# Two-block attention: the parts of the first block's row maxima made by three sums over one tile

## The chip, the cores and the metric

The kernel runs on one core of one Trainium2 chip. The core has a matrix engine (TensorE; PE in the profile, PEld for its weight loads), a vector engine (VectorE, DVE), a scalar engine (ScalarE, ACT), a general engine (GpSimd, POOL), and a queue engine (SyncE, SP) that here issues all transfers. The metric is the device time of one execution in microseconds; the median of the runs is compared.

## What is computed

Two independent attention layers, A and B, each on x of 2048 x 512 float32 with 32 heads of 16. A attends causally within a window of 256 tokens, B to all tokens. Cut to what matters:

```
scores = q @ k^T / sqrt(16)                    # per head, 2048 x 2048
A only: scores = where(0 <= i - j < 256, scores, -1e9)
p = softmax(scores);  o = p @ v;  result = o @ wo
out = concat(A's result, B's result) along the last axis
```

## The kernel before

Block 0 (A) and block 1 (B) are each cut into units (b, g, c): 8 groups g of 4 heads by 4 chunks c of 512 query tokens, 32 units a block. For each unit there are four kinds of work.

First the row maxima. `max_item` multiplies queries and keys for two heads into two PSUM banks and DVE reduces them. In block 0 that is, for a tile of 128 queries, a masked copy inside PSUM (L509) and a reduction over 256 keys (L510), or for the first two query tiles a fused operation for each head (L505). In block 1 it is a reduction over 512 keys (L457). The maxima go to a tile `mt`, allocated by `maxima` from a pool of three.

Second, `max_finish` turns the 16 maxima of a row of partitions (4 heads by 4 query tiles) into three bf16 parts whose sum is the negative maximum to float32 accuracy: part 0 is -m rounded, part 1 is what is left, rounded, part 2 is what is left after that. In block 0, and for the first unit of block 1, DVE does this with four operations (L562 to L565) through a float32 tile `nr`; the later 31 units of block 1 do it on POOL (L559, L560, L564, L565). The parts stand in one of two tiles `nmt` of 128 x 2 x 32 bf16, of which 24 columns of each half are used.

Third, `max_rows`: TensorE transposes the parts into PSUM (L579), ACT copies them to SBUF (`ntr`, L581), and two transfers (L586) write them as three extra rows under the queries in `oq`. The keys carry three rows of ones there, so the next product subtracts the maximum by itself.

Fourth, `scores` (L612) multiplies keys and queries with these rows, ACT takes the exponential (L619), POOL zeroes masked corners in block 0 (L629), and `weigh` or `weigh2` (L658, L643) multiplies with the values.

Block 0 also holds the projections of both layers (L212, L340): their results go through ACT (L295), through POOL (L305, L306) and out to DRAM; key and query loads (L370, L386) bring them back by head. POOL also splits weights and inputs (L162).

The order of PE's work in block 0 is a string written out by hand, `ORDER_A`, one letter for each piece: "m" a `max_item`, "t" a `max_rows`, "s" scores, "w" weighing, "g" and "p" projections, "e" maxima of block 1 made ahead. Around it runs a planner, `Model`: it keeps a time for each engine, for each PSUM bank and for the transfers, adds a planned duration for each piece (`M.run("DVE", 1360)` in `max_finish`), chooses PSUM banks by when they are planned to be free, and slots loads and the follow-up work of DVE and POOL into the program where the planned PE time reaches their due time. A unit's last "m" must come after the "t" of the unit before. Block 1 runs on a repeated pattern of the same letters with a fixed step.

Of the kernel before, what the change touches and what calls it, by code (L numbers as in the profile page):

```python
# [11 lines left out]
F32 = mybir.dt.float32  # L12
F32R = mybir.dt.float32r
BF16 = mybir.dt.bfloat16
AF = mybir.ActivationFunctionType
ALU = mybir.AluOpType
AX = mybir.AxisListType
# [3 lines left out]
HG = 4  # L21
# [121 lines left out]
def attention_kernel(ctx: ExitStack, tc: tile.TileContext, xT, wqk, wv, wo, out):  # L143

    nc = tc.nc
    ctx.enter_context(tc.manual_schedule())

    cst = ctx.enter_context(tc.tile_pool(name="cst", bufs=1))
    sb = ctx.enter_context(tc.tile_pool(name="sb", bufs=2))
# [3 lines left out]
    M = Model()  # L153
    ready = {}
    obank = [None]
    ns = 0
    xs, ws, parts, vd, opq, mt, pts, pvt, od, rl, osp = {}, {}, {}, {}, {}, {}, {}, {}, {}, {}, {}
# [84 lines left out]
    mone = cst.tile([128, 2, 128], BF16, name="mone")  # L242
    later = mone.bitcast(mybir.dt.uint16)
    junk = cst.tile([128, 256], BF16, name="junk")
    nmt = [cst.tile([128, 2, 32], BF16, name=f"nm{i}") for i in range(2)]
    opk = [cst.tile([128, HG // 2, S], F32R, name=f"opk{i}") for i in range(2)]
    vt = [cst.tile([128, NT, VP + 16 * i], F32, name=f"vt{i}") for i in range(2)]
    vst = [cst.tile([128, H, VW], F32, name=f"vst{i}") for i in range(2)]
# [4 lines left out]
    def constants():  # L253
        make_identity(nc, ident)
        nc.gpsimd.memset(minus, -1.0)
        nc.gpsimd.memset(wmask, 0.0)
        nc.gpsimd.affine_select(out=wmask[:, 128:], in_=wmask[:, 128:], pattern=[[-1, 128]],
                                compare_op=ALU.is_ge, fill=NEG, base=0, channel_multiplier=1)
        nc.gpsimd.memset(mone, 1.0)
        nc.gpsimd.affine_select(out=mone, in_=mone, pattern=[[0, 2], [1, 128]], compare_op=ALU.is_ge,  # L260
                                fill=zero_fill, base=-1, channel_multiplier=-1)
        nc.vector.memset(ps_all[:, 0], 0.0)
        for v in vst:
            nc.gpsimd.memset(v, 1.0)
        for v in nmt:
            nc.gpsimd.memset(v, 0.0)
        nc.gpsimd.memset(vt[1][:, :, VP:], 1.0)

# [164 lines left out]

    def maxima(b, g, c):

        if (b, g, c) not in mt:
            m = sb.tile([128, NQC, HG, 4], F32, name=f"mt_{b}_{g}_{c}",
                        **(dict(tag="mte", bufs=1) if (b, g, c) == (1, 0, 0) else dict(tag="mt", bufs=3)))
            mt[b, g, c] = m.rearrange("p k h q -> p h q k")
        return mt[b, g, c]  # L440
# [41 lines left out]
    def max_item(b, g, c, qt, j, kc):  # L482
        n = f"{b}_{g}_{c}_{qt}_{j}_{kc}"
        if b:
            banks, two = take2()
            release2(banks, max2(g, c, qt, kc, (j, j + 1), two))
            return
        m = maxima(b, g, c).rearrange("p (a r) q k -> p a r q k", a=2)
        r = j // 2
        i = 4 * c + qt  # L490
        follow(("k", b, g))
        follow(("q", b, g, c))


        t0, t1 = 128 * max(i - 2, 0), 128 * (i + 1)
        w = t1 - t0
        banks, two = take2()
        for a in range(2):
            rows = slice(ROW[a], ROW[a] + KS)
            nc.tensor.matmul(two[:, a, 0:w], opq[b, g, c][rows, r, 128 * qt:128 * qt + 128], opk2(g)[rows, r, t0:t1],  # L500
                             start=True, stop=True)
        t = M.pe("h", 20 + w / 2.4, loaded(b, g, c))
        if i < 2:
            for a in range(2):
                op = nc.vector.tensor_tensor_reduce(junk[:, :w], two[:, a, 0:w], wmask[:, 256 - w:], 1.0, -3.0e38,  # L505
                                               ALU.add, ALU.max, accum_out=m[:, a, r, qt, 0:1])
                t = M.run("DVE", w / 0.96 + 310, t)
        else:
            nc.vector.copy_predicated(two[:, :, 256:384], later, two[:, :, 0:128])  # L509
            op = nc.vector.tensor_reduce(out=m[:, :, r, qt, 0], in_=two[:, :, 128:384], axis=AX.X, op=ALU.max)  # L510
            M.run("DVE", 455, t)
            t = M.run("DVE", 610)
        release2(banks, mark(op, t))

    def max_chunk(b, g, c, kc):

        n = f"{b}_{g}_{c}"
        m = mt[b, g, c]
        if kc == 1:
            parts["mm"] = sb.tile([128, HG, 4], F32, name=f"mm_{n}", tag="mm")  # L520
        mm = parts["mm"]
        x = m[:, :, :, kc]
        up = sb.tile([128, HG, 4], F32, name=f"mu_{n}_{kc}", tag="mu", bufs=1)
        gt = sb.tile([128, HG, 4], F32, name=f"mg_{n}_{kc}", tag="mg", bufs=1)

        if kc == 1:
            nc.gpsimd.tensor_sub(up, x, m[:, :, :, 0])  # L527
        else:
            nc.gpsimd.tensor_add(up, x, mm)
        nc.gpsimd.tensor_scalar(gt, up, 0.0, None, op0=ALU.is_gt)  # L530
        nc.gpsimd.tensor_mul(up, up, gt)
        if kc == 1:
            nc.gpsimd.tensor_add(up, up, m[:, :, :, 0])
            nc.gpsimd.tensor_scalar(mm, up, -1.0, None, op0=ALU.mult)
        else:
            nc.gpsimd.tensor_sub(mm, mm, up)
        return mm

    def max_finish(b, g, c):

        n = f"{b}_{g}_{c}"
        eng = nc.gpsimd if slot[0] else nc.vector
        m = mt[b, g, c]
        if b == 0:
            mr = m[:, :, :, 0]
        else:
            if slot[0]:
                mr = max_chunk(b, g, c, 3)
            else:
                mr = sb.tile([128, HG, 4], F32, name=f"mm_{n}", tag="mm")  # L550
                nc.vector.tensor_reduce(out=mr, in_=m, axis=AX.X, op=ALU.max)

        nmt.reverse()
        parts["nm"] = nmt[0]
        nm = [nmt[0][:, :, 8 * i:8 * i + 8] for i in range(3)]
        r1 = sb.tile([128, HG, 4], F32, name=f"nr_{n}", tag="nr")
        mr, r1 = (x.rearrange("p (a r) q -> p a (r q)", a=2) for x in (mr, r1))
        if slot[0]:
            eng.tensor_copy(nm[0], mr)  # L559
            eng.tensor_sub(r1, mr, nm[0])  # L560
        else:
            nc.vector.tensor_scalar(nm[0], mr, -1.0, None, op0=ALU.mult)  # L562
            nc.vector.scalar_tensor_tensor(r1, mr, -1.0, nm[0], op0=ALU.mult, op1=ALU.subtract)
        eng.tensor_copy(nm[1], r1)  # L564
        eng.tensor_sub(nm[2], r1, nm[1])  # L565
        ready["nm", b, g, c] = M.run("DVE", 1360)

    def max_rows(b, g, c):
        n = f"{b}_{g}_{c}"
        nm = parts["nm"]  # L570
        if slot[0]:

            bank = M.take("e")
            ps = view(bank)
        else:
            bank, ps = room()
        ps = ps.bitcast(BF16)
        for a in range(2):
            nc.tensor.transpose(ps[32 * a:32 * a + 32, :128], nm[:, a], ident)  # L579
        nt = sb.tile([64, 128], F32, name=f"ntr_{n}", tag="ntr")  # L580
        op = nc.scalar.activation(nt, ps[:64, :128], AF.Copy)  # L581
        t = mark(op, M.run("ACT", 200, M.pe("c", 80)))
        release(bank, t)
        for a in range(2):
            ready["q", b, g, c] = M.dma(12, t)
            nc.sync.dma_start(opq[b, g, c][ROW[a] + KS:ROW[a] + KM].bitcast(F32).rearrange(  # L586
                "s r (q t) -> s (r q) t", t=128), nt[32 * a:32 * a + 24])


    def steps_of(c):  # L590
# [223 lines left out]
    slot = [False, 0]  # L814
# [166 lines left out]
    nm = k = nb = ne = 0  # L981
# [20 lines left out]
    while todo_a or gen[0]:  # L1002
        settle()
        pe = M.t["PE"]
        tl, name = loads()
# [4 lines left out]
        x = "p" if gen[0] else todo_a[0]  # L1010
# [4 lines left out]
        i, j = divmod(ns, HG)  # L1015
        t = NEVER
        if gen[0]:
            t = pe
        elif x == "p":
            t = max(bank(), operands(its_a[nb]))  # L1020
        elif x == "g" and stage == 0:
            t = max(bank(1), operands(its_a[nb]), operands(its_a[nb + 1], int(its_a[nb][0] == its_a[nb + 1][0])))
        elif x == "g":
            t = min(since)[0] if CHUNK * stage == 12 else pe
        elif x == "t" and nts:
            t = max(ready["nm", *nts[0]] + LOAD, bank())
        elif x == "w" and k < i:
            un, (m, pieces), a, z = flat[k]
            t = max(*(ready.get(("v", 0, un[1] // 2, y[0]), NEVER) for y in pieces), ready["p", *un, m] + 100,
                    M.bank("o") if a else 0)  # L1030
        elif x == "s" and i < k + AHEAD and (max_rows, *flat[i][0]) in made:
            t = max(bank(1), ready["q", *flat[i][0]] + LAND)
        elif x == "e":
            t = max(ready.get(("qe",), NEVER), ready.get(("ke", early[ne][2]), NEVER)) + LAND + 1500
            t = max(t, M.pair(), M.t["DVE"] - 300)
        elif x == "m" and not (mxs[nm][2] and (nts or mxs[nm][0][0] and ne < len(early))):
            un, it, z = mxs[nm]
            t = max(*(ready.get(("k", *un[:2], c), NEVER) for c in (range(NQC) if un[0] else range(un[2] + 1))),
                    ready.get(("qd", *un), NEVER)) + LAND
            t = max(t, M.pair())  # L1040
# [25 lines left out]
        elif x == "w":  # L1066
            un, st, a, z = flat[k]
# [74 lines left out]
    ns, nq, nm, half, got = 0, -8, AHEADM, 0, 0  # L1142
# [3 lines left out]
    while nq < 4 * len(steps):  # L1146
# [3 lines left out]
        for x in ORDER if nm < len(mx) else LAST:  # L1150
            k = ns // HG
            if x == "s" and k < len(steps):
                if ns % HG == 0:
                    t = k * STEP
# [88 lines left out]
```

## Time and profile before

| | us |
|---|---|
| median of 3 runs | 1824.5 (1822.27 to 1826.25) |
| the profiled execution | 1817.65 |
| its span, first to last instruction | 1815.8 |
| busy: PE | 1797.3 |
| busy: DVE | 1532.4 |
| busy: ACT | 1398.6 |
| busy: POOL | 648.4 |

The profile is of one execution, with a granted TensorE clock of 0.997 of full speed. A row "PEld x <- DVE y" in a list of waits means that a weight load for x waited for the DVE operation y. In a timeline, the columns are start and duration in us, engine, line, operation, output and input, count, and in brackets the idle time before and what ended it. Matmuls are pipelined and their ends are modelled, so PE counted as busy can still be held back a little.

### The profile page before, as it was taken

To read this page: it belongs to the slowest core of one execution; us is meant where nothing else is said; L and a number is where in the kernel's file an instruction comes from. 1 tells how busy PE (TensorE), PEld (TensorE's weight loads), DVE (VectorE), ACT (ScalarE), POOL (GpSimd) and SP (SyncE) were. 2 spreads that over 40 slices of the span, in tenths; PEclk is the share of its full clock that TensorE was granted. 3 is DMA by queue.
4 is the path that set the end of the run, shared out by engine and by line. 5 is a ranking of instruction groups with operands and counts; after the bars stand their busy time and mean duration, and the time that the engine had idled before them with its cause. 6 is when DMAs were issued, how large, how long until landed. Compare 5 with 4: busy or idle time off the path is not lost.

```text
span 1815.8 us, 39073 instructions
## 1 busy us (share of the span) xinstructions
PE 1797.3 (99%) x14982; PEld 913.6 (50%) x14982; DVE 1532.4 (84%) x2276; ACT 1398.6 (77%) x2750; POOL 648.4 (36%) x1334
## 2 busy tenths in 40 slices
PE   9999999999999999999999999999999999999999
PEld 6776566767764445444444444444444444444436
DVE  5667786777879777799999999999999999999901
ACT  4365666655558777799999999999989999999983
POOL 0367877764654332033310023320112422022330
PEclk9999999999999999999999999999999999999999
DMA  7765667544573221311200221130031121010012
GB/s 246 216 187 201 202 197 224 169 154 145 162 208 105 81 86 55 89 35 40 61 28 27 53 55 29 29 78 16 16 76 34 29 63 37 17 54 11 29 37 93
DMA packets 129162, 166.80 MB, mean 92 GB/s; under 512 B 23012, under 2 KB 58852, under 8 KB 128964
## 3 DMA queue, kind: packets, MB, share of 16 engines
q1 hardware_dynamic: 128976, 164.31, 30.2%
q8 instruction: 118, 1.93, 0.5%
q14 instruction: 68, 0.56, 0.1%
HBM read 94.49 MB, written 68.19 MB: 90 GB/s over the span
## 4 chain that ended last, share of the span: by engine, by line
PE 95%; DVE 2%; ACT 1%; DMA 1%; issue 0%; SPq 0%; POOL 0%; ACTq 0%; DVEq 0%
PE ps_all L643 30%; PE ps_all L453 20%; PE ps_all L612 19%; PE ps_all L212 13%; PE ps_all L340 6%; PE ps_all L658 4%; PE ps_all L500 3%; DVE mt L510 1%; ACT p L619 1%; DVE ps_all L509 0%; DVE mt L457 0%; PE ps_all L579 0%; DMA in<-xT_A 0%; DVE nm L562 0%; DMA opk<-parts 0%
## 5 line engine op out<-in xcount | busy, mean ns | idle before, releaser
L619 ACT ACTIVATE p<-ps_all 128x512 f32<-128x512 f32 x2432 | 1257.9, 597 | 188.2 <-PE ps_all L612 133.3
L457 DVE TENSOR_REDUCE mt<-ps_all 128x2 f32<-128x1024 f32 x1516 | 1195.0, 873 | 62.2 <-PE ps_all L453 55.0
L612 PE MATMUL ps_all<-oq,opk 51*128 51x512 f32 (+2 forms) x2752 | 774.0, 406 | 4.7 <-ACT p L619 2.6
L453 PE MATMUL ps_all<-opk,oq 48*128 48x512 f32 x2016 | 676.1, 439 | 0.4 <-DVE mt L457 0.3
L643 PE MATMUL ps_all<-p,vt 128*17 128x256 f32 (+1 forms) x6056 | 588.6, 461 | 0.6 <-ACT ou L669 0.5
L612 PEld LDWEIGHTS ps_all<-oq,opk 51*128 51x128 f32 x2752 | 398.7, 185 | 183.6 <-ACT p L619 156.2
L453 PEld LDWEIGHTS ps_all<-opk,oq 48*128 48x128 f32 x2016 | 309.7, 185 | 317.4 <-DVE mt L457 179.4
L629 POOL TENSOR_SCALAR_AFFINE_SELECT p<-p 128x256 f32<-128x256 f32 x480 | 178.6, 407 | 109.9 <-ACT p L619 103.7
L643 PEld LDWEIGHTS ps_all<-p,vt 128*17 128x17 f32 x6056 | 100.7, 95 | 223.7 <-issue 213.0
L527 POOL TENSOR_TENSOR mu<-mt 128x16 f32<-128x16 f32 x31 | 6.8, 220 | 508.0 <-DVE mt L457 508.0
L509 DVE COPY_PREDICATED ps_all<-mone,ps_all 128x256 f32<-128x256 uint16 x224 | 95.1, 425 | 82.8 <-PE ps_all L500 80.2
L510 DVE TENSOR_REDUCE mt<-ps_all 128x2 f32<-128x512 f32 x224 | 155.2, 693 | 7.7
L697 POOL TENSOR_TENSOR rd<-ld,minus 128x32 f32<-128x32 f32 x15 | 81.9, 5458 | 219.5 <-DMA ld<-od 219.5
L340 PE MATMUL ps_all<-x,w 64*128 64x512 f32 x672 | 119.3, 392 | 0.0
L212 PE MATMUL ps_all<-x,w 128*128 128x512 f32 x432 | 108.8, 400 | 1.3 <-ACT x L161 1.0
L500 PE MATMUL ps_all<-opk,oq 48*128 48x384 f32 (+2 forms) x512 | 95.1, 370 | 5.0 <-DVE mt L510 2.1
L658 PE MATMUL ps_all<-p,vt 128*17 128x384 f32 (+2 forms) x1408 | 96.4, 389 | 0.0
L212 PE MATMUL ps_all<-w_o,x_o 128*128 128x512 f32 x384 | 92.6, 396 | 0.0
L212 PEld LDWEIGHTS ps_all<-x,w 128*128 128x128 f32 x432 | 78.6, 188 | 24.2 <-issue 3.0
L340 PEld LDWEIGHTS ps_all<-x,w 64*128 64x128 f32 x672 | 85.8, 185 | 6.6 <-ACT raw L295 0.3
L295 ACT ACTIVATE raw<-ps_all 128x512 f32<-128x512 f32 x56 | 32.5, 597 | 72.5 <-PE ps_all L212 55.9
L212 PEld LDWEIGHTS ps_all<-w_o,x_o 128*128 128x128 f32 x384 | 70.6, 188 | 29.6 <-issue 12.8
(82 smaller groups left out, 980.1 us busy)
## 6 DMA issues: line engine op xcount, KB each, us to landing
parts<-st SPq DMA_DIRECT2D x64, 512.0 KB
oq<-parts SPq DMA_DIRECT2D x128, 128.0 KB
opk<-parts SPq DMA_DIRECT2D x128, 128.0 KB
od<-ou SPq DMA_DIRECT2D x64, 256.0 KB
vd<-vst SPq DMA_DIRECT2D x32, 272.0 KB
oq<-parts SPq DMA_DIRECT2D x128, 64.0 KB
opk<-parts SPq DMA_DIRECT2D x128, 64.0 KB
t<-od SPq DMA_DIRECT2D x32, 256.0 KB
```

What stands on the lines that cost most here:

```text
L212: nc.tensor.matmul(ps, l(u), r(v), start=start and k == 0, stop=stop and k == n - 1)
L340: op = nc.tensor.matmul(view(banks[a ^ turn]), l(u)[rows], r(v)[rows], start=turn == q == 0, stop=turn == 1 and q == 11)
L453: nc.tensor.matmul(ps[:, n], q[rows, 128 * qt:128 * qt + 128], k[rows, kc * QC:kc * QC + QC], start=True, stop=True)
L457: op = nc.vector.tensor_reduce(out=m[:, a:a + len(heads), r, qt, kc], in_=ps, axis=AX.X, op=ALU.max)
L500: nc.tensor.matmul(two[:, a, 0:w], opq[b, g, c][rows, r, 128 * qt:128 * qt + 128], opk2(g)[rows, r, t0:t1], start=True, stop=True)
L509: nc.vector.copy_predicated(two[:, :, 256:384], later, two[:, :, 0:128])
L510: op = nc.vector.tensor_reduce(out=m[:, :, r, qt, 0], in_=two[:, :, 128:384], axis=AX.X, op=ALU.max)
L612: nc.tensor.matmul(ps[x][:, col:col + n1], opk2(g)[rows, pr, 128 * k:128 * k + 128], opq[b, g, c][rows, pr, q0:q0 + n1], start=True, stop= ...
L619: op = nc.scalar.activation(p[:, a0 + x, :w], ps[x][:, :w], AF.Exp, scale=SCALE)
L629: nc.gpsimd.affine_select(out=v, in_=v, pattern=[[0, 2], [sign, 128]], compare_op=ALU.is_ge, fill=zero_fill, base=base, channel_multiplier ...
L643: nc.tensor.matmul(o[32 * j:32 * j + VW, q0:q1], vt[(g // 2) % 2][:, kt, vc:vc + VW], pts[1, g, c, kt, j // 2][:, j % 2, q0:q1], start=kt ...
L658: nc.tensor.matmul(o[32 * j:32 * j + VW, q0:q0 + w], vt[(g // 2) % 2][:, kt, vc:vc + VW], pts[b, g, c, m, j // 2][:, j % 2, col:col + w], ...
```

## The change

For block 0, `maxima` no longer allocates a tile of its own: the maxima are written into the first of four slots of a float32 tile `xt` (two of them, used in turn, of 128 x 2 halves x 4 slots x 8). The three parts are bf16 and are written into the upper half-words of the other three slots, whose lower half-words were zeroed once, so that each slot, read as float32, is exactly its part. On DVE part i is then one reduction: the negated sum over slots 0 to i, rounded to bf16. The 31 units of block 1 that finish on POOL keep their four operations and only write into the slots. The transposes read the upper half-words of all four slots (32 columns, every second half-word), and the two transfers take rows 8 to 31 of each half in place of 0 to 23. The planned duration of a finish goes from 1360 to 620 ns.

```diff
-    nmt = [cst.tile([128, 2, 32], BF16, name=f"nm{i}") for i in range(2)]
+    xt = [cst.tile([128, 2, 4, 2 * HG], F32, name=f"nm{i}") for i in range(2)]
...
     def maxima(b, g, c):
 
+        if not b:
+            if (b, g, c) not in mt:
+                xt.reverse()
+                mt[b, g, c] = xt[0]
+            return mt[b, g, c].rearrange("p a s (r q) -> p a r q s", q=4)
...
-        m = maxima(b, g, c).rearrange("p (a r) q k -> p a r q k", a=2)
+        m = maxima(b, g, c)
...
     def max_finish(b, g, c):
 
         n = f"{b}_{g}_{c}"
-        eng = nc.gpsimd if slot[0] else nc.vector
-        m = mt[b, g, c]
-        if b == 0:
-            mr = m[:, :, :, 0]
+        if b:
+            xt.reverse()
+        x = xt[0] if b else mt[b, g, c]
+        parts["nm"] = x
+        nm = x.bitcast(BF16).rearrange("p a s (n u) -> p a n s u", u=2)[:, :, :, :, 1]
+        if slot[0]:
+            mr = max_chunk(b, g, c, 3)
+            r1 = sb.tile([128, HG, 4], F32, name=f"nr_{n}", tag="nr")
+            mr, r1 = (y.rearrange("p (a r) q -> p a (r q)", a=2) for y in (mr, r1))
+            nc.gpsimd.tensor_copy(nm[:, :, :, 1], mr)
+            nc.gpsimd.tensor_sub(r1, mr, nm[:, :, :, 1])
+            nc.gpsimd.tensor_copy(nm[:, :, :, 2], r1)
+            nc.gpsimd.tensor_sub(nm[:, :, :, 3], r1, nm[:, :, :, 2])
         else:
-            if slot[0]:
-                mr = max_chunk(b, g, c, 3)
-            else:
-                mr = sb.tile([128, HG, 4], F32, name=f"mm_{n}", tag="mm")
-                nc.vector.tensor_reduce(out=mr, in_=m, axis=AX.X, op=ALU.max)
-
-        nmt.reverse()
-        parts["nm"] = nmt[0]
-        nm = [nmt[0][:, :, 8 * i:8 * i + 8] for i in range(3)]
-        r1 = sb.tile([128, HG, 4], F32, name=f"nr_{n}", tag="nr")
-        mr, r1 = (x.rearrange("p (a r) q -> p a (r q)", a=2) for x in (mr, r1))
-        if slot[0]:
-            eng.tensor_copy(nm[0], mr)
-            eng.tensor_sub(r1, mr, nm[0])
-        else:
-            nc.vector.tensor_scalar(nm[0], mr, -1.0, None, op0=ALU.mult)
-            nc.vector.scalar_tensor_tensor(r1, mr, -1.0, nm[0], op0=ALU.mult, op1=ALU.subtract)
-        eng.tensor_copy(nm[1], r1)
-        eng.tensor_sub(nm[2], r1, nm[1])
-        ready["nm", b, g, c] = M.run("DVE", 1360)
+            if b:
+                nc.vector.tensor_reduce(out=x[:, :, 0], in_=mt[b, g, c].rearrange("p (a r) q k -> p a (r q) k", a=2),
+                                        axis=AX.X, op=ALU.max)
+            x = x.rearrange("p a s n -> p a n s")
+            with nc.allow_low_precision(reason="a part is what is left, rounded; the sum is float32"):
+                for i in range(3):
+                    nc.vector.tensor_reduce(out=nm[:, :, :, i + 1], in_=x[:, :, :, 0:i + 1], axis=AX.X, op=ALU.add,
+                                            negate=True)
+        ready["nm", b, g, c] = M.run("DVE", 620)
 
     def max_rows(b, g, c):
         n = f"{b}_{g}_{c}"
-        nm = parts["nm"]
+        nm = parts["nm"].bitcast(BF16).rearrange("p a s (n u) -> p a (s n) u", u=2)[:, :, :, 1]
...
-                "s r (q t) -> s (r q) t", t=128), nt[32 * a:32 * a + 24])
+                "s r (q t) -> s (r q) t", t=128), nt[32 * a + 8:32 * a + 32])
```

More of the change, by code (lines that the diff above doesn't have):

```diff
@@ L264, in constants @@
             nc.gpsimd.memset(v, 1.0)
-        for v in nmt:
+        for v in xt:
             nc.gpsimd.memset(v, 0.0)
```

## The prediction

> **What bounds the kernel now.** I read the page first: the span, then the chain that ended last.
>
> ```profile
> span 1815.8 us, 39073 instructions
> ...
> PE 95%; DVE 2%; ACT 1%; DMA 1%; issue 0%; SPq 0%; POOL 0%; ACTq 0%; DVEq 0%
> ```
>
> TensorE (PE) sets the end, so DVE time is worth something only where PE stands waiting for it. The changed lines run on DVE 33 times, from 46.7 to 521.6 us. I therefore read the windows by stretch next: the first block, and the later half of the second.
>
> ```profile
> 45.00:525.00 480.00, 470.73 (x4193) 329.73 (x4193) 350.17 (x740) 278.66 (x566) 321.22 (x621) 1.00 0.60 188
> 1130.00:1735.00 605.00, 604.66 (x5207) 245.56 (x5203) 597.98 (x771) 547.05 (x1071) 148.89 (x351) 1.00 0.14 37
> ```
>
> Columns: stretch, length, busy PE, PEld, DVE, ACT, POOL, then the granted clock. In the first block PE is idle 480.00 - 470.73 = 9.27 us and DVE has 130 us free. In the second PE is idle 0.34 us in 605 although DVE is full (597.98); there the parts are made on POOL. So only the first block can gain, and not much. The waits say for whom: the PEld rows are those of 45 to 525 us, the PE rows those of 45 to 530:
>
> ```profile
> PEld ps_all L612 <- ACT p L619: 13.1, 27, 1.1
> PEld ps_all L500 <- ACT p L619: 9.4, 27, 1.0
> PEld ps_all L500 <- DVE mt L510: 7.6, 19, 0.9
> PE ps_all L500 <- DVE mt L510: 2.1, 5, 0.6
> PE ps_all L612 <- DVE mt L510: 0.7, 2, 0.5
> PE ps_all L612 <- DVE mt L457: 0.6, 1, 0.6
> PEld ps_all L500 <- DVE nm L565: 1.1, 3, 0.4
> PEld ps_all L612 <- DVE nm L565: 0.7, 2, 0.4
> ```
>
> The numbers are the total, the count and the longest in us. A weight load waits (PEld) until a PSUM bank is free; PE itself goes idle only once the earlier matmuls have drained. Idle PE is therefore the low reading of a stall and waiting PEld the high one. DVE is one of two suppliers of banks; ACT is the other.
>
> **The four operations removed.** Their rows, grouped by line and shape:
>
> ```profile
> L562 DVE TENSOR_SCALAR nm<-mt 128x16 bf16<-128x16 f32 x32 | 13.1, 409 | 1.2
> L565 DVE TENSOR_TENSOR nm<-nr,nm 128x16 bf16<-128x16 f32 x33 | 11.1, 336 | 1.1
> L563 DVE SCALAR_TENSOR_TENSOR nr<-mt,nm 128x16 f32<-128x16 f32 x32 | 9.8, 306 | 1.1
> L564 DVE CAST nm<-nr 128x16 bf16<-128x16 f32 x33 | 8.9, 271 | 1.1
> ...
> L551 DVE TENSOR_REDUCE mm<-mt 128x16 f32<-128x64 f32 x1 | 0.3, 269 | 0.0
> ```
>
> 409 + 306 + 271 + 336 = 1322 ns for a unit. The view by tile gives the spread of one of them (shortest, median, longest in ns):
>
> ```profile
> L564 DVE CAST nm<-nr x33: 174/176/1137, 47.2 to 520.2; 128x16 bf16<-128x16 f32 x33
> ```
>
> An operation of 174 ns that can take 1137 waits for something, and the surplus is a wait that shows in no wait row. The timeline of the last of the 33 shows it:
>
> ```profile
> 518.29 1.29 POOL L306 TENSOR_TENSOR st<-raw,st 128x512 fp32r<-128x512 f32 x1
> 518.73 0.27 DVE L551 TENSOR_REDUCE mm<-mt 128x16 f32<-128x64 f32 x1
> 519.04 0.57 DVE L562 TENSOR_SCALAR nm<-mm 128x16 bf16<-128x16 f32 x1
> ...
> 520.21 1.30 POOL L306 TENSOR_TENSOR st<-raw,st 128x512 fp32r<-128x512 f32 x1
> 520.40 1.15 DVE L565 TENSOR_TENSOR nm<-nr,nm 128x16 bf16<-128x16 f32 x1
> ```
>
> Both removed operations shown end 0.03 to 0.04 us after the POOL instruction that was running when they began: L562 at 519.61 behind one ending at 519.58, L565 at 521.55 behind 521.51. The one reduction from SBUF, L551, began and ended inside a POOL instruction and took 0.27: it was not held.
>
> **The three sums added.** No row shows a sum over SBUF. They read 16, 32 and 48 elements a partition and write 16. From below each costs the 174 ns of the smallest operation; from above the 269 ns of L551, which reads 64 with a stride. Near that row, I take 200, 220 and 240 ns: 660 for a unit, with ends 522 and 807. Starts stand about 0.04 us after ends in these rows, so the chain is 4 x 0.04 + 1.32 = 1.48 us before and 3 x 0.04 + 0.66 = 0.78 after. That is 0.70 us a unit, 23 us of DVE time over 33 units, most of it lying in DVE's free 130 us.
>
> The Trainium skill bears on the row L551: the page SBUF — State Buffer, section "Who interferes with whom", says that on trn2 a tensor_reduce never contends with GpSimd for the port the two share, while scalar operations and casts can, and an operation with two SBUF inputs does against a GpSimd instruction that reads SBUF. By that rule the sum is as it stands; by its opposite it is that of the third rival. This case's trace agrees with the rule at its one reduction (0.27 us under a POOL instruction).
>
> **What of it lies on the path.** I looked along the chain of waits for the removed lines. They are on it as a run four times, the last being the one shown (519.04 to 521.55 us). For the other three, the chain's first row and its first after the run, or its last:
>
> ```profile
> 168.29 1.07 DVE nm L562
> ...
> 170.35 0.43 DVE ps_all L509
> ...
> 241.67 0.19 DVE nm L562
> ...
> 243.81 0.35 DVE ps_all L509
> ...
> 338.50 1.08 DVE nm L562
> ...
> 340.37 0.27 DVE nm L565
> ```
>
> The weight loads that came late behind them:
>
> ```profile
> 171.55 0.19 PEld L500 LDWEIGHTS ps_all<-opk,oq 48*128 48x128 f32 x2 [0.60 <-DVE mt L510]
> ...
> 172.61 0.19 PEld L500 LDWEIGHTS ps_all<-opk,oq 48*128 48x128 f32 x2 [0.87 <-DVE mt L510]
> ...
> 243.96 0.19 PEld L612 LDWEIGHTS ps_all<-oq,opk 51*128 51x128 f32 x2 [0.35 <-DVE nm L565]
> ...
> 244.93 0.19 PEld L500 LDWEIGHTS ps_all<-opk,oq 48*128 48x128 f32 x2 [0.79 <-DVE mt L510]
> ...
> 342.64 0.30 PEld L612 LDWEIGHTS ps_all<-oq,opk 51*128 51x128 f32 x4 [0.85 <-DVE mt L510]
> ```
>
> For the fourth, the waits of 515 to 530 us:
>
> ```profile
> PEld ps_all L612 <- DVE mt L457: 0.9, 1, 0.9
> PEld ps_all L453 <- DVE nm L562: 0.4, 1, 0.4
> ```
>
> By waiting PEld the four stalls are 1.47, 1.14, 0.85 and 1.3 us. The runs of removed operations are 2.06, 2.14, 2.14 and 2.51 us; less 0.78 each, the change takes away 1.28, 1.36, 1.36 and 1.73. The smaller of each pair adds to 1.28 + 1.14 + 0.85 + 1.3 = 4.6 us. By PE's own idle time all stalls on DVE in the block are 2.1 + 0.7 + 0.6 = 3.4 us; I put four fifths of it, 2.7, behind these runs as the low end. Elsewhere L565 holds weight loads for 1.1 + 0.7 - 0.35 = 1.45 us; I count a quarter, 0.4. Sum: 5.0 us, with 2.7 and 6.1 as ends if nothing else moves.
>
> **The rest, at nothing.** The maxima of a unit now land in one of two tiles that the parts share; a unit's first maximum must not overwrite parts that TensorE still has to transpose. The source keeps the transposes of a unit ahead of the last maximum of the next in PE's order, so that wait is over before it is asked. The transposes read every second half-word in place of a dense row:
>
> ```profile
> L579 PEld LDWEIGHTS <-nm 128*32 128x32 bf16 x128 | 6.5, 94 | 18.0 <-POOL nm L565 12.0 <-issue 4.4
> ...
> L559 POOL CAST nm<-mm 128x16 bf16<-128x16 f32 x31 | 6.1, 197 | 2.1
> L534 POOL TENSOR_SCALAR mm<-mu 128x16 f32<-128x16 f32 x31 | 8.0, 258 | 2.7
> ```
>
> Element counts stay. In the second block POOL makes the same four operations with a strided output: if each rose from the 197 ns of the cheapest row to the 258 of the dearest POOL row of that shape, that is 4 x 61 = 244 ns in 31 units, 7.6 us, and the transposes do wait there for POOL (12.0 us). I take 0, as these rows look like a fixed cost per instruction; nothing suggests a gain. For the transposes of both blocks I take 0 by their own row: the same 128x32 a load. Doubled, 94 ns on 128 loads are 12 us of weight loading, but PEld is busy only 329.73 of 480 us and loads ahead of PE, so a tenth of it, 1 us, is the upper end. The two transfers of the rows start at partition 8 in place of 0, at equal size: 0. The planner now counts 620 ns in place of 1360 for a finish. PE's list in the first block is written out, but loads, subtractions and stores are slotted in, and PSUM banks chosen, by the planner's clock. They will move a little in either direction; I take 0 and keep the bounds in the rivals.
>
> The profiled execution took 1817.65 us (span 1815.8, 1.85 around it), so by its own time the sum is 1812.65. It lies 6.9 below the median 1824.5 of the runs shown; off that median: 1819.5.
>
> **Rivals.** *More comes free, 1813.* Each finish ends 0.7 us earlier also where DVE's delay reaches PE only after several maxima. All weight-load waits on mt in L500 are 7.6 us, of which 1.47 + 0.79 = 2.3 are in the sum; freeing the other 5.3 and the rest of L565's gives 5.0 + 5.3 + 1.1 = 11.4. Against it: most of those 19 waits stand in stretches of the chain without the removed lines.
>
> *ACT takes the place, 1822.5.* The waits on ACT p L619 (13.1 and 9.4 us) interleave with those on DVE; a bank freed sooner only lets PE reach the next ACT wait. Then the low reading, 2.7, shrinks to about 2. For it: ACT waits are more than DVE's; against it: the late rows quoted name DVE alone.
>
> *The sums are held by POOL too, 1823.3.* Then they keep three quarters of 1.32, and the gain is a quarter of 5.0, about 1.2. Against it stands L551, though it is a single row.
>
> *The planner's shift makes transfers late: slower, 1830.* Place: the key and query loads of the first block, issued on SP between others. The chain has one already:
>
> ```profile
> 288.22 2.69 DMA opk<-parts
> ```
>
> One such landing on the path costs 2.69 us; it turns the sign of what can be measured from four on: 4 x 2.69 - 5.0 = +5.8. For it: 33 x 0.74 = 24 us less are planned for DVE, so issue points do shift; against it: PE's own list is fixed and all loads are gated by PE's planned place.
>
> **Numbers.** About 0.2% (3.65 us) is what a measurement of this kernel can tell. Forecast 0.54, of which 0.50 beyond that bound; more comes free 0.12; ACT takes the place 0.12; sums held 0.05; planner 0.17. Faster 0.50 + 0.12 = 0.62, same 0.04 + 0.12 + 0.05 = 0.21, slower 0.17. The likeliest's own range is 1817.5 to 1822. The whole runs from 1815, into the first rival, to 1827: forecast plus the 7.6 us on POOL, which also holds two late transfers (5.4).
>
> **What would show it.** Three DVE reductions of 128x16 for a unit at 0.17 to 0.27 us with hardly any spread, also under POOL instructions; DVE busy in 45 to 525 us lower by some 20 us; PE's idle time there 6 to 7 us in place of 9.3; the second block's length unchanged and begun 4 to 6 us earlier. I am wrong on the price if the sums spread up to 1.2 us, on the path if DVE falls by 20 us and the block's end doesn't move, and on the rest if DMA rows grow in the chain or the POOL rows of the parts exceed 0.22 us.

## The result, and the profile after

| | before | changed |
|---|---|---|
| median of 17 runs, us | 1822.27 (1815.96 to 1829.12) | 1816.58 (1811.55 to 1820.21) |
| ratio of the runs | | 0.9967, 95% interval 0.9955 to 0.998 |
| the profiled execution, us | 1817.65, span 1815.8 | 1815.08, span 1813.4 |

The kernel became faster by 5.7 us, 0.33%; forecast were 5.0, counted from a median of three runs that the longer series puts 2.2 us lower. The time itself, 1816.58, is therefore 2.9 us below the forecast 1819.5: under the likeliest's own range (1817.5 to 1822), inside the whole one (1815 to 1827).

The changed instructions first. The rows of the changed kernel by line and shape; L567 is the line of the three sums, L562 the reduction of the one unit of block 1 (L551 before), L556 to L559 the four operations on POOL:

```profile
L567 DVE TENSOR_REDUCE nm<-nm 128x16 bf16<-128x16 f32 x33 | 5.8, 175 | 1.1
L567 DVE TENSOR_REDUCE nm<-nm 128x16 bf16<-128x32 f32 x33 | 6.3, 191 | 1.1
L567 DVE TENSOR_REDUCE nm<-nm 128x16 bf16<-128x48 f32 x33 | 7.0, 212 | 1.1
...
L582 PEld LDWEIGHTS <-nm 128*32 128x32 bf16 x128 | 6.7, 94 | 18.8 <-POOL nm L559 12.7 <-issue 4.4
...
L556 POOL CAST nm<-mm 128x16 bf16<-128x16 f32 x31 | 6.3, 203 | 2.1
L559 POOL TENSOR_TENSOR nm<-nr,nm 128x16 bf16<-128x16 f32 x31 | 7.0, 225 | 2.5
```

175 + 191 + 212 = 578 ns stand in place of 1322. The view by tile of the same kernel gives their spread, shortest, median and longest of all 99:

```profile
L567 DVE TENSOR_REDUCE nm<-nm x99: 173/191/218, 45.1 to 517.8; 128x16 bf16<-128x16 f32 x33, 128x16 bf16<-128x32 f32 x33, 128x16 bf16<-128x48 f32 x33
```

None was held: the longest of 99 took 218 ns. The timeline, DVE and POOL merged, at the finish whose four operations took longest before:

```profile
336.02 2.53 POOL L162 TENSOR_TENSOR w<-in,w 128x512 fp32r<-128x512 f32 x2 [0.91 <-ACT w L161]
336.32 0.43 DVE L514 COPY_PREDICATED ps_all<-mone,ps_all 128x256 f32<-128x256 uint16 x1 [0.62 <-PE ps_all L505]
336.78 0.69 DVE L515 TENSOR_REDUCE nm<-ps_all 128x2 f32<-128x512 f32 x1
337.51 0.64 DVE L567 TENSOR_REDUCE nm<-nm 128x16 bf16<-128x16 f32 x3
...
339.70 0.43 DVE L514 COPY_PREDICATED ps_all<-mone,ps_all 128x256 f32<-128x256 uint16 x1 [1.54 <-ACT ou L672]
```

The three sums ran from 337.51 to 338.15 while POOL worked from 336.02 to 338.55. The same finish had taken 3.03 us before: it began at 338.50, and its last operation stands in the timeline of before as

```profile
340.37 1.16 DVE L565 TENSOR_TENSOR nm<-nr,nm 128x16 bf16<-128x16 f32 x1
```

The chain, which left DVE there, had shown only 0.27 us of it. In the changed kernel, after the sums DVE waits 1.54 us for others, where before it went straight on to the next masked copy. The windows by stretch of the changed kernel:

```profile
45.00:525.00 480.00, 472.64 (x4201) 330.55 (x4200) 327.39 (x706) 280.50 (x570) 322.06 (x624) 0.99 0.61 189
...
1130.00:1735.00 605.00, 604.79 (x5196) 245.20 (x5195) 594.18 (x766) 547.37 (x1073) 147.32 (x342) 1.00 0.14 37
```

DVE's busy time in the first block fell from 350.17 to 327.39, by 22.8 us; PE's idle time from 9.27 to 7.36. Of PE's idle time the part behind DVE's maxima nearly vanished. Its waits from 45 to 530 us:

```profile
PE ps_all L615 <- ACT p L622: 2.4, 4, 1.0
PE ps_all L505 <- ACT p L622: 1.5, 4, 0.7
PE ps_all L505 <- DMA oq<-parts: 1.0, 2, 0.8
PE ps_all L505 <- DVE nm L515: 0.6, 1, 0.6
```

That is 0.6 us behind DVE in place of 3.4. The total of 7.36 belongs to this execution alone. A second profile of the same kernel, taken with its repetition below, has 480.00 - 470.03 = 9.97 us of idle PE, more than before; again 0.6 us of it stand behind the maxima (and 0.6 behind another DVE line, L301), while 1.7 stand behind the transfer of the rows (`oq<-ntr`):

```profile
45.00:525.00 480.00, 470.03 (x4182) 328.07 (x4181) 324.27 (x704) 277.70 (x565) 319.29 (x620) 0.99 0.61 188
...
PE ps_all L615 <- DMA oq<-ntr: 1.7, 2, 1.4
...
PE ps_all L505 <- DVE nm L515: 0.6, 1, 0.6
```

By the waits of the weight loads the gain is smaller: those on the maxima in L505, 7.6 us before, are still 6.1. Their waits behind ACT barely moved, from 13.1 and 9.4 us to

```profile
PEld ps_all L615 <- ACT p L622: 14.5, 31, 1.1
...
PEld ps_all L505 <- ACT p L622: 9.4, 25, 1.0
...
PEld ps_all L505 <- DVE nm L515: 6.1, 18, 0.9
```

L505 and L515 are the lines L500 and L510 of before, shifted.

The two profiled executions differ by only 2.4 us of span, less than the medians. The granted clock doesn't explain that: its mean was 0.997 in the execution before and 0.998 in the other. Single executions of one kernel scatter by some 1 to 2 us (standard deviation) about the fit given below, so a pair of them can't carry a difference of 5 us. The losses of clock come at different places in each execution. In these windows the first fence is of before, the second of the changed kernel, and the eighth number is the granted clock:

```profile
0.00:45.00 45.00, 40.91 (x184) 30.46 (x185) 24.22 (x52) 19.38 (x33) 3.38 (x16) 0.96 0.78 248
```

```profile
0.00:45.00 45.00, 40.90 (x191) 30.43 (x192) 25.69 (x54) 19.39 (x33) 3.38 (x16) 1.00 0.78 249
45.00:525.00 480.00, 472.64 (x4201) 330.55 (x4200) 327.39 (x706) 280.50 (x570) 322.06 (x624) 0.99 0.61 189
```

Before lost clock ahead of the first finish, the changed kernel not there but inside its first block.

The runs of the experiments, and those of the changed kernel above, have their mean granted clock beside them. Over these 228 runs a clock lower by 0.001 goes with 1.78 us more, fitted within each kernel's runs. The experiments were run in three series (four, four and two kernels in the order of the table), each with the kernel before in the same rounds. There the kernel before had a lower mean clock (0.9945 to 0.9956) than most others (0.9952 to 0.9972). The experiments below are therefore also given "at equal clock": each run less 1778 us times its lost share of the clock, then the mean with its standard error, as a difference to the kernel before in the same rounds.

This column must be read with care, since the clock may be in part the kernel's own doing. Near 435 us PE idled 1.6 to 2.4 us for late transfers in the profiles of three kernels below (four operations on the new tile, sums in four units, sums in eleven), and right behind it the granted clock fell to 0.50. In the nine other profiles PE idled at most 1.5 us there, and the clock stayed at 1.00. Here is the first of the three, then the changed kernel:

```profile
436.15 0.53 PE L505 MATMUL ps_all<-opk,oq 48*128 48x384 f32 x1 [1.86 <-DMA oq<-parts]
...
438.00:440.00 2.00, 2.00 (x18) 0.49 (x16) 0.99 (x2) 1.08 (x2) 0.67 (x2) 0.50 0.73 260
```

```profile
438.00:440.00 2.00, 2.00 (x22) 1.61 (x20) 1.96 (x4) 0.00 (x0) 1.92 (x5) 1.00 0.51 141
```

It isn't so everywhere: near 207 us two kernels idled 1.75 and 1.85 us and kept their clock. Where a stall does lower the clock, the correction takes out a part of what the stall costs, and the ratio of the runs, which leaves the clock in, is the other reading.

### The profile page after: what moved, and what is told of

It is laid out like the page before. It is cut to its first block, busy times and chain, and to the rows that moved or that the text cites. A ratio compares the mean times of both kernels' runs of the same rounds, so it can differ in the third digit from the quotient of the medians.

```text
span 1813.4 us, 39043 instructions
## 1 busy us (share of the span) xinstructions
PE 1795.6 (99%) x14982; PEld 912.2 (50%) x14982; DVE 1508.8 (83%) x2243; ACT 1398.4 (77%) x2750; POOL 649.0 (36%) x1334
## 5 line engine op out<-in xcount | busy, mean ns | idle before, releaser
L646 PE MATMUL ps_all<-p,vt 128*17 128x256 f32 (+1 forms) x6056 | 587.7, 460 | 0.5 <-ACT ou L672 0.5
L646 PEld LDWEIGHTS ps_all<-p,vt 128*17 128x17 f32 x6056 | 100.7, 95 | 223.3 <-issue 212.7
L515 DVE TENSOR_REDUCE nm<-ps_all 128x2 f32<-128x512 f32 x224 | 155.2, 693 | 7.7
L212 PE MATMUL ps_all<-x,w 128*128 128x512 f32 x432 | 109.2, 401 | 1.3 <-DVE x L162 0.7
L505 PE MATMUL ps_all<-opk,oq 48*128 48x384 f32 (+2 forms) x512 | 95.7, 369 | 3.8 <-ACT p L622 1.5
L212 PE MATMUL ps_all<-w_o,x_o 128*128 128x512 f32 x384 | 92.7, 396 | 0.6 <-ACT ob L765 0.6
L212 PEld LDWEIGHTS ps_all<-x,w 128*128 128x128 f32 x432 | 78.8, 189 | 24.7 <-issue 3.3
L212 PEld LDWEIGHTS ps_all<-w_o,x_o 128*128 128x128 f32 x384 | 70.6, 188 | 30.3 <-issue 12.8
```

The source lines that it names most:

```text
L212: nc.tensor.matmul(ps, l(u), r(v), start=start and k == 0, stop=stop and k == n - 1)
L646: nc.tensor.matmul(o[32 * j:32 * j + VW, q0:q1], vt[(g // 2) % 2][:, kt, vc:vc + VW], pts[1, g, c, kt, j // 2][:, j % 2, q0:q1], start=kt ...
```

## The experiments

| kernel | median us (before) | ratio, 95% interval | at equal clock, us |
|---|---|---|---|
| sums, old plan | 1817.59 (1826.24) | 0.9955, 0.9935 to 0.9976 | -5.3 +- 0.6 |
| new plan only | 1821.52 (1826.24) | 0.9975, 0.9956 to 0.9995 | -0.8 +- 0.5 |
| six sums | 1821.23 (1826.24) | 0.9975, 0.9954 to 0.9996 | -2.8 +- 0.5 |
| one sum | 1820.0 (1826.24) | 0.9958, 0.9939 to 0.9977 | -4.7 +- 0.6 |
| four operations, new tile | 1821.71 (1823.34) | 0.9993, 0.9976 to 1.001 | -1.1 +- 0.5 |
| sums in four units | 1820.25 (1823.34) | 0.9985, 0.9968 to 1.0003 | -2.8 +- 0.5 |
| sums in the other 29 | 1820.08 (1823.34) | 0.9975, 0.9959 to 0.9991 | -2.3 +- 0.5 |
| one subtraction more | 1822.36 (1823.34) | 0.9989, 0.9972 to 1.0007 | -0.8 +- 0.6 |
| changed, once more | 1817.64 (1823.81) | 0.9964, 0.9949 to 0.9979 | -3.1 +- 0.5 |
| sums in eleven held units | 1818.81 (1823.81) | 0.9965, 0.995 to 0.9981 | -4.0 +- 0.6 |

**The sums or the plan.** The change has two parts with a time of their own: the instructions, and the figure in the planner.

```diff
-        ready["nm", b, g, c] = M.run("DVE", 620)
+        ready["nm", b, g, c] = M.run("DVE", 1360)
```

> The changed kernel with the planned duration of a finish put back to 1360 ns, so that loads are placed as before. Theory DVE (what a finish takes on DVE is what counts): as the changed kernel, ratio to the kernel before 0.997 (0.995 to 0.999), three sums of about 0.58 us a unit. Rival plan (the moved loads bring the gain): ratio 1.000 (0.9985 to 1.0015).

```diff
-        ready["nm", b, g, c] = M.run("DVE", 1360)
+        ready["nm", b, g, c] = M.run("DVE", 620)
```

> The kernel before with the planned duration of a finish at 620 ns and its four operations unchanged. Theory DVE: ratio 1.000 (0.9985 to 1.0015), finishes still 1.3 us a unit. Rival plan: 0.997 (0.995 to 0.999).

The first has the whole gain, so the sums suffice without the new plan. The second has a ratio of 0.9975 whose interval excludes 1, as the plan's rival would have it; but its runs had a mean clock of 0.9966 against 0.9945, and at equal clock 0.8 +- 0.5 us are left. As the clock may depend on the kernel, a gain of the plan by itself isn't excluded; the gain of the change doesn't need it. The two plans differ in little: PE's instructions stand in one and the same order, though some write to other PSUM banks, one maximum changes place on DVE, and a handful of loads and splits change place on the other queues.

**More and less time on DVE.**

```diff
-                for i in range(3):
+                for i in (0, 1, 2, 0, 1, 2):
```

> The changed kernel with its three sums made twice over: six sums, about 1.16 us and with their gaps 1.4 us a unit, about what the four operations took (1.48) but without their spread of up to 2.5 us. Theory DVE in the form of the prediction's sum (mean time on DVE): the gain is gone, ratio 1.000 (0.999 to 1.001). In the form that the long, held finishes matter and the others don't: about half the gain stays, 0.9985. Rival (the gain has nothing to do with DVE's time): as the changed kernel, 0.997.

```diff
-                for i in range(3):
+                for i in range(1):
```

> The changed kernel with only the first of the three sums in the units that DVE finishes; parts 1 and 2 of these units stay zero, so their maxima are subtracted rounded. DVE saves a further 0.48 us a unit, 16 us over 33. Theory DVE as in the prediction (four stretches, whose stalls are already gone): at most 1.5 us further, ratio 0.996 to 0.997. Rival more-comes-free (DVE's time is on the path all through the first block): a further 16 x 6/23 = 4 us, ratio 0.9945.

Six sums put DVE's busy time of the first block back to 347.05 us, 3 below that of the kernel before:

```profile
45.00:525.00 480.00, 473.27 (x4207) 331.86 (x4207) 347.05 (x808) 279.82 (x570) 322.66 (x623) 1.00 0.62 189
```

Yet half of the gain stays (2.8 of 5.3 us in the same rounds). So DVE's total is not the price; finishes of nearly constant 1.4 us cost about half of what finishes of 0.8 to 3.0 us with the same mean cost. Where that half is lost isn't seen: in this kernel's profile PE idles 0.8 us behind the maxima, hardly more than in the changed one. One sum takes a further 13 us off DVE (314.41 us busy) and gains nothing more: 4.7 +- 0.6 against 5.3 +- 0.6. The rival by which DVE's time pays all through the block, 4 us further, falls.

**The tile.** The four old operations on the new tile, at the old plan; `mr` is the slot of the maxima:

```diff
-                for i in range(3):
-                    nc.vector.tensor_reduce(out=nm[:, :, :, i + 1], in_=x[:, :, :, 0:i + 1], axis=AX.X, op=ALU.add,
-                                            negate=True)
+                nc.vector.tensor_scalar(nm[:, :, :, 1], mr, -1.0, None, op0=ALU.mult)
+                nc.vector.scalar_tensor_tensor(r1, mr, -1.0, nm[:, :, :, 1], op0=ALU.mult, op1=ALU.subtract)
+                nc.vector.tensor_copy(nm[:, :, :, 2], r1)
+                nc.vector.tensor_sub(nm[:, :, :, 3], r1, nm[:, :, :, 2])
```

> The new tile, its strided parts, the transposes of every second half-word and the transfers from row 8, but DVE makes the parts with the four old operations, planned at 1360 ns. Theory DVE: as the kernel before, which at an equal granted clock is 5.2 us above the changed one; ratio 1.000 (0.9985 to 1.0015) at equal clock. Rival layout (the tile shared by maxima and parts is what gains): as the changed kernel, 0.997.

Ratio 0.9993; at equal clock 1.1 +- 0.5 us, two standard errors from nothing. The tile by itself gains about a fifth of the 5.3 us, with nothing and two fifths as ends, and the strided transposes and the transfers from row 8 cost nothing that shows.

**Which finishes.** Both of these, at the old plan and on the new tile, take four operations in some units and three sums in the rest, by a condition on (b, g, c) around the two forms. Units are counted from 0; the four are 8, 14, 21 and 32.

```diff
+            if (b, g, c) not in ((0, 2, 0), (0, 3, 2), (0, 5, 1), (1, 0, 0)):
...
+            else:
```

> As the first of these, but the three sums in four units alone, those whose four operations stood on the chain of waits of the profile before (units 8, 14, 21 and 32 of the 33); the other 29 keep four operations. Theory of the prediction (the gain lies in those four stretches, 4.6 of 5.0 us): 4 to 5 us below the kernel with four operations everywhere, at equal clock. Rival (the gain is spread over all finishes by their held time): the four units hold 6.7 of the 24 us taken off DVE, so 1.4 us.

```diff
+            if (b, g, c) in ((0, 2, 0), (0, 3, 2), (0, 5, 1), (1, 0, 0)):
```

> The opposite: three sums in the other 29 units, four operations in units 8, 14, 21 and 32. Theory of the prediction: 0.4 to 1 us below the kernel with four operations everywhere, at equal clock. Rival spread: 3.8 us below.

Neither theory fits both. At equal clock the four units bring 2.8 us below the kernel before (1.7 +- 0.6 below four operations everywhere), the other 29 bring 2.3 (1.2 +- 0.6). The first lies near the rival's 1.4, not the 4 to 5 of the prediction; the second near the prediction's 0.4 to 1, not the rival's 3.8. By this measure the four are worth about half, at an eighth of the finishes. The ratios of the runs, 0.9985 and 0.9975 against 0.9993, give them less, with intervals that overlap. PE's waits of the kernel with sums in those four:

```profile
PE ps_all L505 <- DMA oq<-parts: 1.6, 2, 1.2
PE ps_all L623 <- DVE nm L570: 1.4, 1, 1.4
PE ps_all L505 <- DVE nm L515: 1.1, 3, 0.6
```

L570 is the last of the four operations where they remain, and by this list PE stood 1.4 us behind one of them, that of unit 11:

```profile
206.33 0.64 DVE L570 TENSOR_TENSOR nm<-nr,nm 128x16 bf16<-128x16 f32 x1
...
207.08 0.78 PE L623 MATMUL ps_all<-oq,opk 51*128 51x128 f32 x4 [1.39 <-DVE nm L570]
```

This finish took only 1.28 us (1.95 in the profile before). The same four score matmuls stood still for 1.5 us in the kernel with sums in the other 29 and for 1.7 in the changed kernel's second profile, there behind the transfer of the rows, while the three sums had long ended. So it isn't settled that the finish held PE here. The longest finish, that of unit 16, took 3.3 us in place of 2.0 and left no idle PE: the granted clock was 0.50 from 272 to 276 us, and twelve matmuls of L212 kept PE busy for 5.08 us in place of 3.06. The first operation of unit 16 is the longest here (shortest, median, longest):

```profile
L567 DVE TENSOR_SCALAR nm<-nm x29: 178/182/2394, 47.0 to 493.3; 128x16 bf16<-128x16 f32 x29
```

The next question was whether the length of the hold picks the units better than the chain of one execution does. The lengths themselves mostly recur: the eleven finishes that took 1.9 us or more before did so again in the kernel with four operations on the new tile.

```diff
+            if (b, g, c) not in ((0, 1, 1), (0, 1, 3), (0, 2, 0), (0, 2, 3), (0, 3, 2), (0, 4, 0), (0, 4, 1), (0, 5, 0), (0, 5, 1), (0, 6, 0), (1, 0, 0)):
```

The first expectation is for the changed kernel once more, as it stands and in the same rounds; the second is for this edit, at the old plan.

> The changed kernel once more, on the chip and in the rounds of the next one, so that partial versions have a whole to be measured against. All theories: 4.5 to 6 us below the kernel before at equal granted clock, ratio 0.997.

> Three sums in the eleven units alone whose four operations took 1.9 us or more in the profile before (units 5, 7, 8, 11, 14, 16, 17, 20, 21, 24, 32; first start to last end), four operations in the other 22; planned at 1360 ns. Theory held (what counts is how long POOL holds a finish): these units hold 17.2 of the 25.6 us of the surplus over three sums, and the long ones are those that reach TensorE, so 80 to 100% of the gain: 4 to 5.2 us below the kernel before at equal clock. Theory of the prediction (four stretches, all among the eleven): 4.6 us, no less. Rival (each finish pays alike, by the number of its operations): 11 of 33, so 1.7 us.

Sums in a third of the units bring the whole gain, within the errors: 0.9965 against 0.9964 of the changed kernel in the same rounds, at equal clock 4.0 +- 0.6 against 3.1 +- 0.5. The rival by number of operations, 1.7 us, lies far below 4.0 +- 0.6; with the tile's 1.1 us counted apart it comes to 1.1 + (5.2 - 1.1) / 3 = 2.5 us, which is made unlikely and not excluded. The changed kernel's own 3.1 lies below its expectation of 4.5 to 6. The sums with the old plan had 5.3 in the first series; either a difference is uncertain by more than the half microsecond of its formal error, or the new plan takes something off. No series has both. In the units where POOL happens to stand still, four operations cost about what three sums do, as this timeline of the kernel before shows:

```profile
194.48 0.17 DVE L562 TENSOR_SCALAR nm<-mt 128x16 bf16<-128x16 f32 x1
194.69 0.18 DVE L563 SCALAR_TENSOR_TENSOR nr<-mt,nm 128x16 f32<-128x16 f32 x1
194.90 0.17 DVE L564 CAST nm<-nr 128x16 bf16<-128x16 f32 x1
195.10 0.17 DVE L565 TENSOR_TENSOR nm<-nr,nm 128x16 bf16<-128x16 f32 x1
```

That is 0.79 us from first start to last end, against 0.65 for three sums.

**Who holds whom.** To see the hold by itself, one operation of the old kind was put behind the sums:

```diff
+            nc.vector.tensor_sub(spare, xt[0][:, :, 0], minus[:, 0:16].rearrange("p (a n) -> p a n", a=2))
```

> The changed kernel with one more DVE instruction behind the sums of each of the 33 units: a subtraction of two SBUF tiles of 128x16 float32 into a tile that nobody reads. Theory port (a DVE operation with two inputs from SBUF is held until the running POOL instruction ends, a reduction isn't): the sums keep 0.17 to 0.22 us each; the subtraction takes 0.17 us when POOL stands still and up to 1.3 us otherwise, mean 0.3 to 0.6 us. Rival (it was the chain of four through a separate tile that waited): the subtraction too takes 0.17 to 0.22 us always. Time at equal clock 0.5 to 2.5 us above the changed kernel by the first, under 0.5 by the second.

The view by tile of the subtraction:

```profile
L570 DVE TENSOR_TENSOR spare<-nm,minus x33: 161/169/4098, 48.0 to 525.4; 128x16 f32<-128x16 f32 x33
```

The sums in front of it kept 173 to 220 ns. The subtraction took 161 to 4098, and the timeline of the longest, DVE, POOL and PE merged, shows behind whom:

```profile
267.15 0.65 DVE L568 TENSOR_REDUCE nm<-nm 128x16 bf16<-128x16 f32 x3
267.46 1.29 POOL L162 TENSOR_TENSOR x<-in,x 128x512 fp32r<-128x512 f32 x1
267.71 4.10 DVE L570 TENSOR_TENSOR spare<-nm,minus 128x16 f32<-128x16 f32 x1
268.70 1.85 POOL L634 TENSOR_SCALAR_AFFINE_SELECT p<-p 128x256 f32<-128x256 f32 x5
270.52 1.26 POOL L162 TENSOR_TENSOR x<-in,x 128x512 fp32r<-128x512 f32 x1
271.73 0.42 DVE L515 COPY_PREDICATED ps_all<-mone,ps_all 128x256 f32<-128x256 uint16 x1
...
272.93 0.61 PE L506 MATMUL ps_all<-opk,oq 48*128 48x384 f32 x3 [2.21 <-DVE nm L516]
```

It was held from 267.71 to 271.81, through seven POOL instructions in a row, until POOL's last ended at 271.78; PE then stood idle 2.21 us for the next maximum. That a subtraction is held behind POOL and a sum is not is shown. That a hold ends with the running instruction is true of most: of the 15 subtractions that took over 0.2 us, 12 ended behind the first POOL instruction that ended, two behind the second and this one behind the seventh. Of the 69 such operations in the kernel before, 68 ended behind the first, and in 58 of these POOL had by then begun its next. The finish at 338.50 has one of them: L565 ended at 341.53, behind the POOL instruction that ended at 341.50, though the next had begun at 341.44:

```profile
340.18 1.32 POOL L306 TENSOR_TENSOR st<-raw,st 128x512 fp32r<-128x512 f32 x1
341.44 2.56 POOL L629 TENSOR_SCALAR_AFFINE_SELECT p<-p 128x256 f32<-128x256 f32 x7
```

What lets one operation in and keeps another out for seven instructions isn't shown. By itself that one event costs what was forecast for all 33 subtractions (0.5 to 2.5 us); the kernel lost about 2.3 us or more of the changed kernel's gain (3.1 to 5.3 in the other rounds, 0.8 +- 0.6 left).

## Why the prediction came out right, point by point

*What bounds.* PE, and its stalls behind DVE in the first block alone. Shown: the last half of the second block is unchanged (PE idle 0.34 and 0.21 us of 605), and PE's idle time behind DVE's maxima in the first went from 3.4 to 0.6, in both profiles of the changed kernel.

*The hold.* Shown, by 99 sums without spread and by the one subtraction. The Trainium skill's rule (SBUF — State Buffer, "Who interferes with whom"), that a reduction doesn't contend for the port shared with GpSimd and an operation with two SBUF inputs does, agrees with this case's traces: 218 ns at the longest of 99, against 4098. No trace here shows the port itself. The rival that the sums are held too falls.

*The sums.* 660 ns were put down and 578 measured; both inside the ends 522 and 807. DVE fell by 22.8 us where 23 were forecast. The upper bound taken from L551 was too careful, since that row has 64 elements.

*What lies on the path.* The sum of 5.0 is right within what the runs can tell; its two terms are not, so that the sum came out is in part luck. The four stretches of the chain were sized at 4.6 us and measured at 1.7 to 2.8 (below four operations on the new tile, and below the kernel before); the other finishes, "a quarter, 0.4", at 1.2 to 2.3. The step that failed is taking the four stretches of one chain for nearly the whole price. What the runs show in its place is a gain spread over more finishes; why the four carry only about half stays open. Eleven finishes chosen by the length of the hold, the four among them, carry all of it within the errors. One reading was off without effect: the third run of removed operations took 3.03 us and not 2.14, but the stall behind it, 0.85, was the term.

*The parts put at nothing.* POOL's four operations rose from 197 to 203 ns a copy and from 218 to 225 ns for the last subtraction, just past the 0.22 us named as a sign of being wrong; the waits of the transposes on them went from 12.0 to 12.7 us, and nothing of it reached the end. The strided loads stayed at 94 ns. The tile by itself: 1.1 +- 0.5 us faster at equal clock. The plan by itself: 0.8 +- 0.5 at equal clock, more by its ratio.

*The rivals.* More comes free: excluded by the single sum. ACT takes the place: the weight loads' waits on it grew by 1.4 us, while PE's own idle time behind DVE shrank by 2.8 and the gain stayed. Late transfers by the new plan: the kernel that has the plan alone idled 1.5 us behind loads in place of 1.1, and the changed one 1.0, far from what would turn the sign. The 1.7 us behind the rows' transfer in the changed kernel's second profile need not be of the plan: the kernel with sums in the other 29, on the old plan, has 1.5 there.

*What would show it.* The sums without spread and DVE's 20 us came. The other two signs did not: PE's idle time was 7.4 in one profile and 10.0 in the other, not 6 to 7, and the second block's weighing (L643 before, L646 after) began at 536.6 us in the one and at 541.0 in the other, where before it began at 539.4, and not 4 to 6 us earlier. Each of these includes what its execution lost in clock.

## What to carry to other kernels

A DVE operation that takes 0.17 us in one place and 1.1 in another, with no wait shown, should be laid beside POOL's timeline: if it ends 0.03 us after a POOL instruction, as here, it was held, and the time is booked as its own duration. An operation that isn't held can be worth more than its saving in mean time where another engine waits in line behind it; here six unheld sums cost half of what four held operations of the same mean did. And the stalls counted along one chain gave the sum better than the places.

## What was not expected of the hardware

A DVE subtraction of 16 elements a partition was once held for 4.10 us behind seven POOL instructions that followed each other closely, where most holds ended with the first. And the spread of this kernel's runs is largely that of the granted clock, 1.78 us for each 0.001. The clock falls to 0.50 for some 3.4 us or twice that at a time, and in eleven of the twelve profiles one such fall lies between 242 and 275 us. Kernels whose instructions stand in nearly the same order differ by a ratio of 0.9975 in their runs and by 0.8 +- 0.5 us at equal clock.
